# Gated mix of two linear attentions on one core: all projections as seven products of quadrant sums, in three passes over the tokens

## The chip, the cores and the metric

One core of a Trainium2 chip. The metric is the device time of one execution in microseconds (us). Before the change it is 582.25 us, the median of 3 runs (582.17 to 582.32).

## What is computed

x has 2048 tokens of 576 features, all numbers are float32. There are 32 heads of 18. Both branches project x to queries, keys and values, run a linear attention without a mask, and project to 576 outputs; a gate per token mixes the two.

```
g = sigmoid((x * gate_w).sum(-1))
A: q, k, v = x @ A_wqkv;  pq, pk = phi(q), phi(k)      phi(t) = (t > 0 ? t + 1 : exp(t)) + 1e-6
B: q, k, v = x @ B_wqkv;  pq, pk = per head [softmax(t @ w_phi), softmax(-t @ w_phi)]
both:  kv = sum over tokens of pk^T v;  z = sum of pk
       o = (pq @ kv) / (pq . z + 1e-6);  y = o @ wo
out = g * yA + (1 - g) * yB
```

So there are two phases: keys and values of all tokens, then queries and outputs of all tokens.

## The kernel before, in words

**Precision.** Each float32 operand of a projection or output product is split into a high part (rounded to the fast matmul type) and a low part. A product is x_hi W_hi + x_hi W_lo + x_lo W_hi. The 576 features are four chunks of 128 and a tail of 64, whose high and low parts of the weight share the 128 rows of a fifth chunk. One projection is therefore 4 x 3 + 2 = 14 matmuls (`proj`, lines 479 to 486), the token tile (128 x 128) being the loaded operand and up to 512 weight columns the streamed one.

**Tiles and loops.** Tokens are worked in 16 tiles of 128 (`NT`). The branch weights stand in two large tiles `WA` and `WB` (name `WW`), the query weights of B in `W`, those of A in `WW` again; `late` holds the last value columns of both branches (`WR`) and later the normalised queries. `load_x` (426 to 434) loads a token tile and splits it. `keys_values` (584 to 590) computes 1008 columns at once, 512 and 496. `fold_group` (456 to 477) multiplies the per-head map w_phi into B's key or query weights; five groups make a set. `kv_pair` (573 to 579) adds the key-value sums of two tiles in PSUM (name `bk`), 44 small matmuls per branch.

**Order of the stages.** Fold B's key weights and project tiles 0 and 1 in pieces (630 to 656); tiles 2 to 13 in the loop from 660; the last two tiles with their queries (874 to 936); then blocks of two tiles in which query projections (`q_units`), normalisation (`norm_a`, `norm_b`), transposes (`tr_units`), numerators (`num`) and output products (`out_units`) of different tiles are woven (946 to 960). A's key-value map is multiplied into its output weights (`ma_units`, 696 to 722), and the pieces are put together in SBUF by small transfers.

**Who does what.** PE: matmuls and transposes. ACT: copies out of PSUM with rounding, and exponentials. DVE: low parts, maxima, subtractions, sums, reciprocals. POOL: low parts of x, scaling. SP: issues almost all transfers, in order.

**What sets the order.** Operations aren't issued as they are written. A planner (class `Plan`, 139 to 350) records them, gives each a cost (`weigh`, 199 to 230), a due time from the order of the PE work, and picks for each engine the operation with the earliest due time among those that could start soon (`run`, 266 to 339), with the free buffers of each tile name counted in. It then emits them all from line 349, so every instruction in the profile has that line, and groups are told apart by tile names. PSUM holds two tiles of two banks (`pq`), two `tr` and two `bk`.

Of the kernel before, what the change touches and what calls it, by code (L numbers as in the profile page):

```python
# [18 lines left out]
P = 128  # L19
S, D, H, DH = 2048, 576, 32, 18  # L20
NT = S // P
KT = 5
HB = 288
GH = 7
GROUPS = [(g, min(GH, H - GH * g)) for g in range(5)]
NPAIR = 6
# [4 lines left out]
KV = D + 24 * DH  # L31
# [5 lines left out]
class View:  # L37
# [31 lines left out]
    def cells(self):  # L69

        n = math.prod(self.tile.shape[1:])
        first, last = int(self.idx.min()) // n, int(self.idx.max()) // n
        return np.stack([self.idx[0] + (q - first) * n for q in range(first // 32 * 32, last + 1, 32)])
# [23 lines left out]
class Tile:  # L97
    bases = {}

    def __init__(self, pool, shape, dtype, kw):  # L100
        self.pool, self.shape, self.dtype, self.kw = pool, tuple(shape), dtype, kw
        self.psum = pool.psum
# [14 lines left out]
class Pool:  # L117
    def __init__(self, plan, name, real, bufs, psum=False):
        self.plan, self.name, self.real_pool, self.bufs, self.psum = plan, name, real, bufs, psum
# [234 lines left out]
def tile_gated_mix(ctx, tc, xT, wAk, wAv, wBv, wR, wAq, wkT, wqT, phi, woA, woB, out):  # L354
# [9 lines left out]
    ps = Pool(plan, "ps", ctx.enter_context(tc.tile_pool(name="ps", bufs=2, space=bass.MemoryType.PSUM)), 2, True)  # L364

    def r(ap):
        return ap.bitcast(F32)

    def pq_tile():
        return ps.tile([P, 2, 512], F32, name="pq")  # L370

    def tr_tile():
        return ps.tile([P, 512], F32, name="tr")
# [4 lines left out]
    def row_tile():  # L378
        return wk.tile([P, 640], F32, name="row", bufs=6)

    def wraw_tile():
        return wk.tile([P, 640], F32, name="wraw", bufs=3)

    def uw_tile():
        return wk.tile([P, 2, D], F32, name="uw", bufs=3)
# [5 lines left out]
    wr = warm.bitcast(F32R)  # L391
# [26 lines left out]
    z_b = cst.tile([P, 2, D], F32, name="z_b")  # L418
    kb = cst.tile([UB, NB, 64], F32, name="kb")
# [6 lines left out]
    def load_x(t, parts=()):  # L426
        raw = wk.tile([P, 640], F32, name="xraw").rearrange("p (j n) -> p j n", n=P)
        xh = wk.tile([P, KT, P], F32R, name="xh")
        xl = wk.tile([P, KT, P], F32R, name="xl")
        for j in parts or [slice(0, KT)]:  # L430
            SP.dma_start(raw[:, j], xT[t, :, j])
            A.activation(xh[:, j], raw[:, j], AF.Copy)
            (V if parts else G).tensor_tensor(xl[:, j], raw[:, j], r(xh[:, j]), op=ALU.subtract)
        return xh, xl


    def w_tile():
        return wp.tile([P, 9, 578], F32R, name="W", bufs=1)

    def two_tile():  # L440
        return wp.tile([P, 2 * 9 * 578], F32R, name="WW")

    def split(src, hi, lo, eng=V, raw=None):
        raw = (wraw_tile() if raw is None else raw)[:src.shape[0], :src.shape[1]]
        SP.dma_start(raw, src)
        A.activation(hi, raw, AF.Copy)
        a = P - lo.shape[0] if hi.shape[0] == P else 0
        eng.tensor_tensor(lo, raw[a:], r(hi[a:]), op=ALU.subtract)

    def load_w(src, W, n, eng=V, raws=(None,) * KT):  # L450
        for j in range(4):
            split(src[:, j, :], W[:, j, :n], W[:, 5 + j, :n], eng, raws[j])
        split(src[:, 4, :], W[:, 4, :n], W[64:, 4, :n], eng, raws[4])
        return W

    def fold_group(src, W, ph, g, raw=None, tr=False):

        n = GROUPS[g][1] * DH
        rows = P if g < 4 else 80
        raw = wraw_tile() if raw is None else raw  # L460
        SP.dma_start(raw[:rows], src[g, :rows])
        yield
        if tr:
            p1, p2 = tr_tile(), tr_tile()
        else:
            pq = pq_tile()
            p1, p2 = pq[:, 0], pq[:, 1]
        for i in range(KT):
            dst = p1[:, 126 * i:126 * i + n] if i < 4 else p2[:, :n]
            PE.matmul(dst, raw[:n, P * i:P * i + P], ph[:n, 126 * g:126 * g + n], start=True, stop=True)  # L470
        p1v = p1[:, :504].rearrange("p (i c) -> p i c", c=126)[:, :, :n]
        c = slice(126 * g, 126 * g + n)
        A.activation(W[:, 0:4, c], p1v, AF.Copy)
        A.activation(W[:, 4, c], p2[:, :n], AF.Copy)
        V.tensor_tensor(W[:, 5:9, c], p1v, r(W[:, 0:4, c]), op=ALU.subtract)
        V.tensor_tensor(W[64:, 4, c], p2[64:, :n], r(W[64:, 4, c]), op=ALU.subtract)
        yield

    def proj(dst, x, W, c0, n):
        xh, xl = x  # L480
        steps = []
        for j in range(4):
            steps += [(xh, j, j), (xh, j, 5 + j), (xl, j, j)]
        steps += [(xh, 4, 4), (xl, 4, 4)]
        for i, (xx, j, w) in enumerate(steps):
            PE.matmul(dst, xx[:, j, :], W[:, w, c0:c0 + n], start=(i == 0), stop=(i == len(steps) - 1))
# [8 lines left out]
    def phi_elu(pq):  # L495
# [4 lines left out]
        A.activation(fv, pq, AF.Relu, bias=epsc, scale=-1.0)  # L500
        A.activation(fx, fx, AF.Exp, bias=epsc, scale=-1.0)
        V.scalar_tensor_tensor(fv, pq, EPS, fv, op0=ALU.max, op1=ALU.add)
        return f

    def softmax_exp(pq):
        mm = sm.tile([P, 64], F32, name="mm")
        V.tensor_reduce(mm[:, :32], heads(pq), op=ALU.max, axis=AX.X)
        V.tensor_reduce(mm[:, 32:], heads(pq), op=ALU.min, axis=AX.X)
        uw = uw_tile()
# [4 lines left out]
        V.tensor_tensor(v4(0), heads(pq), bc2(mm[:, :32]), op=ALU.subtract)  # L514
        V.tensor_tensor(v4(1), bc2(mm[:, 32:]), heads(pq), op=ALU.subtract)
# [26 lines left out]

    vt = []
    for i in range(4):
        if i < 2:
            v = wk.tile([P, 2, 640], F32, name="ath").rearrange("p a c -> p (a c)")[:, :22 * VC]
            v = v.rearrange("p (a g c) -> p a g c", a=2, c=VC)
        else:
            v = wk.tile([P, 2, 11, VC], F32, name="vo")
        G.memset(v[:, :, 10:, 2 * DH:], 0.0)  # L550
        G.memset(v[:, :, :, 3 * DH:], 1.0)
        vt.append(v)
    kv = [bank_tile(), bank_tile()]

# [3 lines left out]
    def kv_group(t, which, gr, dst, rhs, first):  # L558
        PE.matmul(dst, vt[t % 4][:, which, gr, :], rhs, start=(t == 0 and first), stop=(t == NT - 1), skip_group_check=True)

    def kv_a(t, f):
        for gr, nh in GRP3:
            p, a = divmod(gr, 2)
            kv_group(t, 0, gr, kv[0][64 * a:64 * a + VC, 54 * p:54 * p + DH * nh], f[:, 54 * gr:54 * gr + DH * nh], p == 0)

    def kv_b(t, uw):
        for gr, nh in GRP3:
            p, a = divmod(gr, 2)
            b, o = b_region(p)
            kv_group(t, 1, gr, kv[b][64 * a:64 * a + VC, o:o + 2 * DH * nh].rearrange("p (s c) -> p s c", s=2),  # L570
                     uw[:, :, 54 * gr:54 * gr + DH * nh], p == 1)

    def kv_pair(pend):
        with plan.piece():
            for t, f, _ in pend:
                kv_a(t, f)
            for t, _, u in pend:
                kv_b(t, u)
        pend.clear()

    def evac_v(t, which, src):
        A.activation(vt[t % 4][:, which, :8, :54], src.rearrange("p (g c) -> p g c", c=54), AF.Copy)

    def keys_values(t, x, W, which):

        pq = pq_tile().rearrange("p a c -> p (a c)")
        proj(pq[:, :512], x, W, 0, 512)
        proj(pq[:, 512:KV], x, W, 512, KV - 512)
        evac_v(t, which, pq[:, D:KV])
        return pq[:, :D].rearrange("p (a c) -> p a c", a=2)  # L590

    def last_values(t, x):

        pv = tr_tile()
        proj(pv[:, :HB], x, WR, 0, HB)
        pv = pv[:, :HB].rearrange("p (a c) -> p a c", a=2)
        A.activation(vt[t % 4][:, :, 8:10, :54], pv[:, :, :108].rearrange("p a (g c) -> p a g c", c=54), AF.Copy)
        A.activation(vt[t % 4][:, :, 10, :36], pv[:, :, 108:], AF.Copy)

    def a_part(t, x):  # L600
        return phi_elu(keys_values(t, x, WA, 0))

    def b_part(t, x):
        uw, rs = softmax_exp(keys_values(t, x, WB, 1))
        scale_uw(uw, rs, G)
        last_values(t, x)
        return uw

    xs = {}

    WB, WA = [two_tile()[:, :9 * KV].rearrange("p (j n) -> p j n", j=9) for _ in range(2)]
    WR = wk.tile([P, 2600], F32R, name="late", bufs=1)[:, :9 * HB].rearrange("p (j n) -> p j n", j=9)
# [418 lines left out]
```

## Time and profile before

| | |
|---|---|
| median of 3 runs | 582.25 us |
| the profiled execution | 584.05 us |
| its span, first to last instruction | 582.3 us |
| granted TensorE clock | 1.000 |
| DVE, ACT, POOL busy | 329.7, 230.7, 186.5 us |
| moved by DMA | 29.05 MB |

Groups in the profile read: line, engine, operation, output tile <- input tiles, shapes, count, then busy time, mean of one, and idle time before them with what ended it. Matmul records cover the pipeline from entry to end, so neighbouring records overlap and the means are longer than the distance between two starts.

### The profile page before, as it was taken

Reading aid. Unit: us, or ns where it says so; the run is one execution under the profiler, and the core shown is the slowest. Engines: PE = TensorE matmul, PEld = TensorE weight load, DVE = VectorE, ACT = ScalarE, POOL = GpSimd, SP = SyncE. Lnnn points to the kernel's source line nnn. Section 1 sums busy time; section 2 is a strip of 40 time slices with the busy share of each in tenths; the row PEclk is TensorE's granted clock in tenths of the full one; section 3 lists DMA queues with packets and bytes.
Section 4 is the critical chain, followed back from the end, with each engine's and each line's share of the span. In section 5 each row is a group of like instructions: output and inputs, shape, how many; then the busy total and the mean of one; then the engine's idle time right before and its main releaser. Section 6 shows DMA issues by size and latency. Waiting matters only on the chain.

```text
span 582.3 us, 10081 instructions
## 1 busy us (share of the span) xinstructions
PE 574.1 (99%) x4180; PEld 522.5 (90%) x4180; DVE 329.7 (57%) x553; ACT 230.7 (40%) x486; POOL 186.5 (32%) x154
## 2 busy tenths in 40 slices
PE   7999999999999999999999999999999999999997
PEld 7978888888888888888889899999999999999997
DVE  3951443324333332353479998777778787787610
ACT  4643332323333231324366543535444444533531
POOL 4031221212222121247264664342334333333200
PEclk9999999999999999999999999999999999999999
DMA  8631101111000000002144101011011010000001
GB/s 296 213 106 44 46 24 24 35 44 43 26 23 24 12 14 21 24 25 82 46 112 131 57 22 44 24 44 44 20 45 44 24 44 22 21 22 20 4 38 42
DMA packets 15014, 29.05 MB, mean 50 GB/s; under 512 B 2508, under 2 KB 4812, under 8 KB 14968
## 3 DMA queue, kind: packets, MB, share of 16 engines
q1 hardware_dynamic: 14824, 28.33, 15.9%
q8 instruction: 33, 0.54, 0.4%
q14 instruction: 13, 0.11, 0.1%
q10 hardware_dynamic: 144, 0.06, 0.0%
HBM read 22.65 MB, written 4.72 MB: 47 GB/s over the span
## 4 chain that ended last, share of the span: by engine, by line
PE 89%; DVE 4%; DMA 4%; ACT 2%; SPq 1%; issue 0%
PE pq L349 52%; PE bk L349 25%; PE tr L349 12%; DMA row<-wkT 1%; DMA wraw<-wAk 1%; ACT WW L349 1%; DVE late L349 1%; DVE WW L349 1%; SPq L349 1%; DMA wraw<-wAv 1%; DVE den L349 1%; DMA wraw<-woB 1%; DVE mm L349 0%; DVE uw L349 0%; DVE row L349 0%
## 5 line engine op out<-in xcount | busy, mean ns | idle before, releaser
L349 PE MATMUL pq<-WW,xh 128*128 128x512 f32 (+3 forms) x864 | 243.7, 358 | 0.3 <-DVE WW L349 0.3
L349 PEld LDWEIGHTS pq<-WW,xh 128*128 128x128 f32 x864 | 153.1, 188 | 21.5 <-DVE WW L349 0.8
L349 PE MATMUL pq<-WW,xl 128*128 128x512 f32 (+3 forms) x480 | 169.7, 356 | 0.0
L349 POOL TENSOR_TENSOR xl<-xraw,xh 128x640 fp32r<-128x640 f32 x30 | 47.0, 1566 | 177.4 <-ACT xh L349 175.4
L349 PEld LDWEIGHTS pq<-WW,xl 128*128 128x128 f32 x480 | 90.4, 188 | 12.0
L349 DVE TENSOR_REDUCE mm<-pq 128x32 f32<-128x576 f32 x64 | 45.6, 752 | 85.5 <-ACT vo L349 43.8
L349 PE MATMUL bk<-WW,vo 128*128 128x288 f32 x480 | 70.8, 296 | 0.0
L349 PEld LDWEIGHTS bk<-WW,vo 128*128 128x128 f32 x480 | 65.8, 188 | 0.0
L349 PE MATMUL pq<-W,xh 128*128 128x288 f32 x288 | 63.2, 303 | 0.0
L349 DVE SCALAR_TENSOR_TENSOR row<-pq,row 128x576 f32<-128x576 f32 x32 | 24.1, 753 | 67.5 <-ACT ath L349 23.8
L349 DVE TENSOR_REDUCE ss<-uw 128x64 f32<-128x1152 f32 x32 | 43.1, 1348 | 26.3 <-ACT uw L349 26.2
L349 PE MATMUL bk<-WW,ath 128*128 128x288 f32 x256 | 55.9, 305 | 0.0
L349 POOL TENSOR_TENSOR uw<-uw,rs 128x1152 f32<-128x1152 f32 x16 | 34.4, 2154 | 48.6 <-DVE rs L349 48.6
L349 PEld LDWEIGHTS pq<-W,xh 128*128 128x128 f32 x288 | 47.3, 189 | 0.5
L349 ACT ACTIVATE row<-pq,epsc 128x576 f32<-128x576 f32 x32 | 23.8, 744 | 58.2 <-PE pq L349 58.2
L349 ACT ACTIVATE uw<-uw 128x1152 f32<-128x1152 f32 x32 | 37.3, 1165 | 23.8 <-DVE uw L349 23.8
L349 PE MATMUL pq<-W,xl 128*128 128x288 f32 x160 | 46.5, 296 | 0.0
L349 PEld LDWEIGHTS bk<-WW,ath 128*128 128x128 f32 x256 | 40.6, 188 | 2.7 <-issue 2.7
L349 ACT ACTIVATE uT<-tr 118x512 f32<-118x512 f32 (+1 forms) x44 | 24.6, 564 | 44.0 <-PE tr L349 44.0
L349 POOL TENSOR_TENSOR row<-row,den 128x378 f32<-128x378 f32 (+1 forms) x32 | 29.4, 939 | 36.7 <-DVE den L349 29.5
L349 POOL TENSOR_TENSOR row<-uw,z_b 128x576 f32<-128x576 f32 x18 | 26.6, 1482 | 40.3 <-ACT uw L349 23.1
L349 PE MATMUL bk<-WW,atl 128*128 128x288 f32 x128 | 37.7, 294 | 0.0
(119 smaller groups left out, 822.5 us busy)
## 6 DMA issues: line engine op xcount, KB each, us to landing
xraw<-xT SPq DMA_DIRECT2D x30, 320.0 KB
out<-row SPq DMA_DIRECT2D x15, 288.0 KB
wraw<-woB SPq DMA_DIRECT2D x6, 288.0 KB
wraw<-wAq SPq DMA_DIRECT2D x5, 289.0 KB
wraw<-wAk SPq DMA_DIRECT2D x5, 288.0 KB
wraw<-woA SPq DMA_DIRECT2D x5, 288.0 KB
wraw<-wqT SPq DMA_DIRECT2D x4, 320.0 KB
wraw<-wkT SPq DMA_DIRECT2D x3, 320.0 KB
```

The costliest lines, as they stand in the source:

```text
L349: fn(*[a.real() if isinstance(a, View) else a for a in args], **{k: v.real() if isinstance(v, View) else v for k, v in kw.items()})
```

## The change

1. **Seven products.** Tokens are taken in pairs of tiles (t1, t2), features in two halves of 256 and the tail of 64, columns in two matrices k and v (keys and values, or B's and A's queries). A pair's result is a 2 x 2 block product, and `strassen` computes it in seven products of sums of quadrants, accumulated in three PSUM tiles X, Y, Z. The tail is multiplied plainly in four products. Each product runs over two halves of 288 columns (290 in pass A, whose extra columns hold the gate). Kept partial sums are copied out of X by ACT (`keep`) and added to Y or Z by DVE.
2. **Three passes.** Pass A: keys and values of branch A for all tokens, tiles 0 and 1 in the plain form. Pass B: keys and values of branch B. Pass Q: queries of both branches with normalisation, transposes, numerators and output. Each pass uses the operand set of its own; during a pass the next pass's set is prepared (`set_ops`): differences of quadrants, split in high and low. Three of a set's seven operands go through DRAM and are loaded when tiles come free (11 tiles `op`).
3. **x.** `x_prep` (pass A) forms the quadrant sums of x, splits them and stores them in DRAM; `x_load` (passes B, Q) loads them again and splits the plain parts afresh. The tiles xu, xv, xp, xq have one buffer each.
4. **Output weights** are split or computed in pass B, put together in DRAM (`WO_d`) by transfers, and loaded as four `op` tiles and a `tail` in pass Q.
5. **Buffers.** Three `pq` tiles in place of two; `tr` is gone (in pass Q one `pq` tile takes its part); 8 `row` tiles, 2 `uw` tiles. Key-value sums of A and B are separate pieces (`kv_a`, `kv_b`). Planner costs are as they were.
6. **Engines.** The subtractions of the first softmax of a pair are on POOL in pass Q; feature maps and softmaxes read sums in SBUF instead of PSUM in three of the four quadrants in pass Q, and in one of two in passes A and B.

```diff
-        raw = wk.tile([P, 640], F32, name="xraw").rearrange("p (j n) -> p j n", n=P)
...
+    def x_prep(n, raw, sums):
+        x, (xu, xv, xp, xq) = x_tiles()
+        r1, r2 = chunks(raw[:, 0]), chunks(raw[:, 1])
+        s2, s1, s3, s4 = [sums[:, 2 * i:2 * i + 2] for i in range(4)]
+        A.activation(xu[:, 0], r1, AF.Copy)
+        G.tensor_tensor(xu[:, 1], r1, r(xu[:, 0]), op=ALU.subtract)
...
+        V.tensor_tensor(s1, r2[:, 0:2], r2[:, 2:4], op=ALU.add)
+        V.tensor_tensor(s2, s1, r1[:, 0:2], op=ALU.subtract)
...
+        SP.dma_start(XP_d[n], r(xp))
+        SP.dma_start(XQ_d[n], r(xq))
...
+    def x_load(n):
+        for t, src, k in ((xu, xT[2 * n], 5), (xv, xT[2 * n + 1, :, 2:], 3)):
+            raw = chunks(wk.tile([P, 640], F32, name="raw", bufs=1)[:, :P * k])
+            SP.dma_start(raw, src)
+            split(raw, t[:, 0], t[:, 1], G)
+        SP.dma_start(r(xp), XP_d[n])
+        SP.dma_start(r(xq), XQ_d[n])
...
+    def op_steps(x, w):
+        return [s for j in range(2) for s in ((x(0, j), w[:, j]), (x(0, j), w[:, 2 + j]), (x(1, j), w[:, j]))]
+    def tail_steps(x, w):
+        return [(x(0, 0), w), (x(1, 0), w)]
+    def strassen(x, W, T, n, c1_tile, c11, c22, c21, c12):
+        X = pq_tile()
+        mul(X, op_steps(x["11"], W[1]), True)
+        c1 = pair(c1_tile())
+        keep(c1, X, n)
+        Y = pq_tile()
+        mul(Y, op_steps(x["12"], W[2]) + tail_steps(x["t1"], T[:, 0]), True)
+        V.tensor_tensor(c1, c1, Y[:, :, :n], op=ALU.add)
+        c11(c1)
+        mul(X, op_steps(x["s2"], W[6]), False)
+        keep(c2, X, HB)
+        Z = pq_tile()
+        mul(Z, tail_steps(x["t2"], T[:, 1]) + op_steps(x["s1"], W[5]), True)
+        mul(X, op_steps(x["s3"], W[7]), False)
+        keep(c3, X, HB)
+        c22(c3, Z)
+        mul(X, op_steps(x["22"], W[4]) + tail_steps(x["t2"], T[:, 0]), False)
+        c21(X)
+        mul(Z, op_steps(x["s4"], W[3]) + tail_steps(x["d"], T[:, 1]), False)
+        c12(c2, Z)
...
+    def b_sinks(n, uws, pend):
+        t1, t2 = 2 * n, 2 * n + 1
+        return (lambda c: softmax_k(t1, c, uws[0], V, pend), lambda c, Z: v_add(t2, c, Z),
+                lambda X: softmax_k(t2, X[:, :, :HB], uws[1], V, pend), lambda c, Z: v_add(t1, c, Z))
...
+        for i, _ in enumerate(strassen(x, WB, TB, D // 2, lambda: uws[0][:, 0], *b_sinks(n, uws, pend))):
+            if i == 3 and n + 1 < NT // 2:
+                x_next = x_load(n + 1)
+            if i == 4:
+                if n:
+                    kv_b(done)
+                else:
+                    kv_a(a_done)
+            if n or i > 4:
+                steps(prep)
...
+    def q_units(n, x, uws, c1_tile, mid=None, end=None):
+        def c11(c):
+            qb[t1] = softmax_exp(c, uws[0], G)
+        def c22(c, Z):
+            V.tensor_tensor(c, c, Z[:, :, :HB], op=ALU.add)
+            qa[t2] = phi_elu(c)
+        def c21(X):
+            qb[t2] = softmax_exp(X[:, :, :HB], uws[1])
+        def c12(c, Z):
+            V.tensor_tensor(c, c, Z[:, :, :HB], op=ALU.add)
+            qa[t1] = phi_elu(c)
```

More of the change, by code (lines that the diff above doesn't have):

```diff
@@ L437, in w_tile @@
[L437 to L454, printed above, removed]
@@ L479, in proj @@
[L479 to L486, printed above, removed]
+    XP_d = [dr.tile([P, 2, 4, P], F32, name=f"xp{n}") for n in range(NT // 2)]
+    XQ_d = [dr.tile([P, 2, 5, P], F32, name=f"xq{n}") for n in range(NT // 2)]
@@ new lines, in load_ops, with folds, load @@
+    def load_ops(W, Wd, x):
+        for op in (7, 4, 3):
+            W[op] = op_tile()
+            plan.first = ()
+            SP.dma_start(r(W[op]), Wd[op])
+    def folds(src, K, ph, raw, ahead):
+        SP.dma_start(ph, phi.rearrange("p a c -> p (a c)"))
+        def load(g):
+            rows = P if g < 4 else 80
+            rw = raw()
+            SP.dma_start(rw[:rows], src[g, :rows])
+            return rw
+        nxt = load(0)
+        yield
+        for g, nh in GROUPS:
+            n = nh * DH
+            rw, nxt = nxt, load(g + 1) if g < 4 and ahead else None
+            pq = pq_tile()
+            for i in range(KT):
+                dst = pq[:, 0, 126 * i:126 * i + n] if i < 4 else pq[:, 1, :n]
+                PE.matmul(dst, rw[:n, P * i:P * i + P], ph[:n, 126 * g:126 * g + n], start=True, stop=True)
+            if g < 4 and not ahead:
+                nxt = load(g + 1)
+            c = slice(126 * g, 126 * g + n)
+            A.activation(K[:, 0:4, c], pq[:, 0, :504].rearrange("p (i c) -> p i c", c=126)[:, :, :n], AF.Copy)
+            A.activation(K[:, 4, c], pq[:, 1, :n], AF.Copy)
+            yield
@@ L672, in widths, with kv_group, kv_order, kv_a @@
-    def widths(p):
-        return [(a, DH * GRP3[2 * p + a][1]) for a in range(2) if 2 * p + a < len(GRP3)]
+    def kv_group(t, gr, dst, rhs, first):
+        PE.matmul(dst, vt[t % 4][:, gr, :], rhs, start=(t == 0 and first), stop=(t == NT - 1), skip_group_check=True)
+    def kv_order(t):
+        return [GRP3[g ^ (t % 2 if g < 10 else 0)] for g in range(11)]
+    def kv_a(pend):
+        with plan.piece():
+            for t, f in pend:
+                for gr, nh in kv_order(t):
+                    p, a = divmod(gr, 2)
+                    kv_group(t, gr, kv[0][64 * a:64 * a + VC, 54 * p:54 * p + DH * nh], f[:, 54 * gr:54 * gr + DH * nh], p == 0)
@@ new lines, in kv_b, with steps @@
+    def kv_b(pend):
+        with plan.piece():
+            for t, uw in pend:
+                for gr, nh in kv_order(t):
+                    p, a = divmod(gr, 2)
+                    b, o = b_region(p)
+                    kv_group(t, gr, kv[b][64 * a:64 * a + VC, o:o + 2 * DH * nh].rearrange("p (s c) -> p s c", s=2),
+                             uw[:, :, 54 * gr:54 * gr + DH * nh], p == 1)
+    def steps(gen, n=1):
+        for _ in range(n):
+            next(gen, None)
+    raw = at_tile([2, 640])
@@ new lines, in tile_gated_mix, with tmp_rows @@
+    (k1, s1), (k2, s2) = plain(1, 2, 0, 0), plain(1, 2, 0, 1)
+    for i in range(0, 10, 2):
+        run(s1[i:i + 2])
+        run(s2[i:i + 2])
+    pend = []
+    for t, k in enumerate((k1, k2)):
+        pend.append((t, phi_elu(k[:, :, :HB])))
+        gate_of(t, k[:, 0, HB:HB + 1])
+    for t in range(2):
+        v, s = plain(12, 3, 1, t)
+        run(s)
+        v_copy(t, v)
+    x_load_raw(1, raw)
+    x = x_prep(1, raw, sums)
+    def tmp_rows():
+        return row_tile()[:, :2 * HG], row_tile()[:, :2 * HG]
@@ new lines, in islice_pair, with drams @@
+    def islice_pair(u):
+        return u[:, 0], u[:, 1]
+    def drams(name):
+        return {op: dr.tile([P, 4, D], F32, name=f"{name}{op}") for op in (7, 4, 3)}
+    WB, WBd, TB = {}, drams("wb"), tail_tile()
+    prep = prep_b()
+    for n in range(1, NT // 2):
+        done, pend = pend, []
+        x_next = None
+        for i, _ in enumerate(strassen(x, WA, TA, HG, row_tile, *a_sinks(n, pend))):
+            if i == 0 and n < NT // 2 - 1:
+                x_load_raw(n + 1, raw)
+            if i == 2 and n < NT // 2 - 1:
+                x_next = x_prep(n + 1, raw, sums)
+            if i == 4:
+                kv_a(done)
+            steps(prep)
+        x = x_next
@@ L675, in runs @@
+    steps(prep, 99)
+    x = x_load(0)
+    load_ops(WB, WBd, x)
+    spare = [at_tile([2048]) for _ in range(2)]
+    more = [s[:, :2 * D].rearrange("p (s n) -> p s n", s=2) for s in spare]
+    ph = spare[1][:, 2 * D:2 * D + 630]
+    rawq = spare[0][:, 2 * D:2 * D + 640]
+    WO_d = dr.tile([P, 2, 9, D], F32, name="wod")
+    MA_d = dr.tile([198, 2, D], F32, name="mad")
     def runs(size):
@@ new lines, in tile_gated_mix, with load_out, WO @@
+    steps(prep, 99)
+    x = x_load(0)
+    load_ops(WQ, WQd, x)
+    def load_out(x):
+        flat = WO_d.rearrange("p s i n -> p (s i) n")
+        for k in range(4):
+            t = op_tile()
+            plan.first = x["dma"][:1]
+            SP.dma_start(r(t), flat[:, 4 * k:4 * k + 4])
+            WOt.append(t)
+        t = tail_tile()
+        plan.first = x["dma"][:1]
+        SP.dma_start(r(t), flat[:, 16:18])
+        WOt.append(t)
+    WOt = []
+    def WO(s, i):
+        c = 9 * s + i
+        return WOt[c // 4][:, c % 4]
@@ new lines, in chain, with end0 @@
+    def chain(*gens):
+        for g in gens:
+            yield from g
+    UBS = []
+    def end0():
+        fold_b()
+        UBS.extend([late[:, 0], late[:, 1]])
+    late = wide_tile(1, [2, 1300])
+    late = late.rearrange("p a c -> p a c")[:, :, :UB * NB]
+    uT = wide_tile(0, [NB, 256])
+    b_done = pend
+    extra_uw = wk.tile([P, 2, D], F32, name="vo")
+    for _ in q_units(0, x, [uw_tile(), uw_tile()], row_tile, lambda: kv_b(b_done), end0):
+        pass
+    blocks = [{} for _ in range(NT // 2 + 3)]
@@ new lines, in tile_gated_mix @@
+    for i in range(NT // 2 + 1):
+        while norms:
+            norms.pop(0)()
+        cur, prev = blocks[i], blocks[i - 1]
+        seqs = []
+        if i and i <= NT // 2:
+            prev["ot"] = num(uT, prev["at"], i >= NT // 2 - 1)
+        if i + 1 < NT // 2:
+            x = x_load(i + 1)
+            if i == 0:
+                load_out(x)
+            uws = [extra_uw if i == 0 else uw_tile(), uw_tile()]
+            seqs.append((7, .7, q_units(i + 1, x, uws, row_tile)))
+        ts = (2 * i + 1, 2 * i)
+        if i < NT // 2:
+            at = at_tile([2, 4, 256], F32R)
+            cur["at"] = (at[:, 0], at[:, 1])
+            seqs.append((8, 1, chain(*[tr_units(t, cur["at"], uT) for t in ts])))
+        if i:
+            seqs.append((4, 1, chain(*[out_units(t, prev) for t in (2 * i - 1, 2 * i - 2)])))
+        merge(*seqs)
```

676 lines of the change are left out of this document (348 added, 328 removed).

## The prediction

> **What bounds the kernel now.** I read the page's busy times first, then the windows over whole periods, then the groups of matmuls, then single rows of the timeline.
>
> ```profile
> PE 574.1 (99%) x4180; PEld 522.5 (90%) x4180; DVE 329.7 (57%) x553; ACT 230.7 (40%) x486; POOL 186.5 (32%) x154
> PE 89%; DVE 4%; DMA 4%; ACT 2%; SPq 1%; issue 0%
> ```
>
> PE is busy for 574.1 of 582.3 us, and 89% of the chain that ended last runs through it. A busy PE is a modelled figure, so I ask the windows whether it works at a steady rate. The first row below is a pair of token tiles in the keys-and-values stage, the second a pair in the query stage (columns: window, then PE, PEld, DVE, ACT, POOL busy with counts, clock, DMA share, GB/s).
>
> ```profile
> 102.70:135.80 33.10, 33.10 (x240) 28.72 (x239) 11.49 (x17) 10.87 (x20) 7.03 (x4) 1.00 0.11 29
> 401.60:437.20 35.60, 35.60 (x278) 34.26 (x274) 27.91 (x49) 16.03 (x38) 12.48 (x11) 1.00 0.11 36
> ```
>
> No idle PE, full clock, DVE at 35% in the first and 78% in the second. So the time is PE's queue of work, and removed PE work comes off the end only if the other four engines keep up with a faster PE.
>
> **The change, part by part.**
>
> *Projection matmuls.* The groups, by shape:
>
> ```profile
> L349 PE MATMUL pq<-WW,xh 128*128 128x512 f32 x270 | 88.6, 398 | 0.3 <-DVE WW L349 0.3
> L349 PE MATMUL pq<-WW,xh 128*128 128x496 f32 x270 | 85.1, 387 | 0.0
> L349 PE MATMUL pq<-W,xh 128*128 128x288 f32 x288 | 63.2, 303 | 0.0
> L349 PE MATMUL pq<-WW,xl 128*128 128x512 f32 x150 | 59.0, 393 | 0.0
> L349 PE MATMUL pq<-WW,xl 128*128 128x496 f32 x150 | 58.1, 387 | 0.0
> L349 PE MATMUL pq<-W,xl 128*128 128x288 f32 x160 | 46.5, 296 | 0.0
> L349 PE MATMUL pq<-WW,xh 128*128 128x288 f32 x180 | 38.1, 297 | 0.0
> L349 PE MATMUL pq<-WW,xh 128*128 128x290 f32 x144 | 32.1, 305 | 0.0
> L349 PE MATMUL tr<-late,xh 128*128 128x288 f32 x144 | 30.3, 296 | 0.0
> L349 PE MATMUL pq<-WW,xl 128*128 128x288 f32 x100 | 28.9, 295 | 0.0
> L349 PE MATMUL pq<-WW,xl 128*128 128x290 f32 x80 | 23.7, 301 | 0.0
> L349 PE MATMUL tr<-late,xl 128*128 128x288 f32 x80 | 23.0, 294 | 0.0
> ```
>
> Their means overlap (a matmul's record covers its pipeline), so I price by the distance between starts. The first column of these timeline rows is the start.
>
> ```profile
> 13.49 0.51 PE L349 MATMUL pq<-WW,xh 128*128 128x288 f32 x2
> 21.00 0.55 PE L349 MATMUL tr<-WW,xh 128*128 128x432 f32 x2
> 26.55 0.42 PE L349 MATMUL tr<-late,xh 128*128 128x288 f32 x2
> 61.97 0.62 PE L349 MATMUL pq<-WW,xh 128*128 128x512 f32 x2
> 68.34 1.28 PE L349 MATMUL tr<-row,wraw 126*128 126x126 f32 x10
> ```
>
> From 13.49 to 21.00 stand four sets of 14 matmuls of 288 columns: 7.51/56 = 0.1341 us each. From 61.97 to 68.34 stand 14 of 512 and 14 of 496: 6.37/28 = 0.2275 us. From 21.00 to 26.55 stand 28 of 432: 5.55 us. The two prices give 0.432 ns a column and about 9.6 ns a matmul.
>
> Before: 840 wide ones are 30 sets of 6.37 = 191.1; 28 of 432 are 5.5; 1176 of 288 or 290 are 157.7, and two more columns on 224 of them 0.2. Sum 354.5 us.
>
> After: a pair of tiles needs, per pass, 7 products of 6 steps by 2 halves, and 4 tails of 2 steps by 2 halves: 84 + 16 = 100 matmuls of 288 or 290 columns. The plain form in the same width is 2 tiles by 14 steps by 4 = 112. Eight pairs by three passes is 24, of which the first is plain: 23 x 100 + 112 = 2412, which is also the count in the changed kernel's own instructions (812 of 290, 1600 of 288). 2412 x 0.1341 + 0.7 = 324.2 us. **Minus 30.3 us.** One product in eight would be 12.5%; the tails, which are not saved, and the narrower matmuls leave 8.5%.
>
> A rule against it: the Trainium skill, TensorE: Matmul & The Clock Gate, section Back-to-back issue gap, gives for sustained streams about 81 ns at 128 columns and 131 ns at 512, so that wide matmuls would be far cheaper per column. By that rule, interpolated, the projections would go from about 230 to about 246 us, an estimate, and the change would lose 13 us or so. The trace does not agree: 227.5 ns against 134.1.
>
> *Start.*
>
> ```profile
> 4.75 2.34 PE L349 MATMUL pq<-row,wraw 126*128 126x126 f32 x10
> 11.27 1.31 PE L349 MATMUL pq<-row 72*128 72x72 f32 x10 [0.60 <-DMA row<-wkT]
> 12.41 1.32 PE L349 MATMUL tr<-row 126*128 126x126 f32 x10
> 4.00:6.00 2.00, 2.00 (x10) 2.00 (x10) 0.00 (x0) 0.00 (x0) 1.19 (x8) 1.00 1.01 361
> 6.00:8.00 2.00, 1.09 (x6) 0.80 (x4) 0.08 (x1) 0.76 (x2) 0.00 (x0) 1.00 1.01 384
> ```
>
> Before, five fold groups (11.27 to 12.41 is 1.14 us each, 5.7 us in all) come first, and projections begin at 13.49. After, the first work is the plain product of pair 0, whose 112 matmuls take 15.0 us. The first load lands at about 4.7 (the 4.75 row), and two splits of about 0.7 us on ACT follow, so it starts near 6.2. Its keys need 2.1 MB, which at 361 to 384 GB/s is in by 8, so PE sets the pace. The folds come back later as 5.7 us of PE work. Net: -13.5 + 6.2 + 5.7 = **-1.6 us**, between -2.5 and +2 (if the splits, not PE, pace it).
>
> *Switches of matmul kind.*
>
> ```profile
> 379.87 0.60 PE L349 MATMUL tr<-ident,late 128*118 128x128 f32 x4
> 380.23 0.51 PE L349 MATMUL pq<-WW,xh 128*128 128x290 f32 x2
> 380.58 0.29 PE L349 MATMUL pq<-WW,xl 128*128 128x290 f32 x1
> 380.71 0.43 PE L349 MATMUL pq<-WW,xh 128*128 128x290 f32 x2
> 380.97 0.30 PE L349 MATMUL pq<-WW,xl 128*128 128x290 f32 x1
> ```
>
> Two matmuls after transposes take 0.35 us (380.23 to 380.58), two in the stream 0.26: a switch costs 0.09. The key-value sums now stand in 16 pieces where 8 stood (A's and B's in different passes), 16 more switches: **+1.4 us**. Transposes, numerators, output products and their counts are unchanged.
>
> So without any new wait: 582.25 - 30.3 - 1.6 + 1.4 = **551.7 us**. The profiled execution took 584.05, its span 582.3; I apply differences to the median of the runs, 582.25.
>
> *New waits.* Nothing in the old trace shows them, so I bound them.
>
> What must now be hidden: per pair, three additions of a kept sum to PSUM (in Q) or one and two value additions (in B), six ACT copies out of PSUM, operand preparation for the next pass on DVE, POOL and ACT, and x re-read through SP's queue (236 transfers in place of 124).
>
> ```profile
> L349 DVE TENSOR_TENSOR uw<-pq,mm x32: 741/749/758, 23.4 to 533.8; 128x576 f32<-128x576 f32 x32
> L349 DVE TENSOR_REDUCE ss<-uw x32: 1293/1353/1354, 33.5 to 536.4; 128x64 f32<-128x1152 f32 x32
> L349 DVE RECIPROCAL rs<-ss x32: 495/545/554, 36.0 to 539.8; 128x64 f32<-128x64 f32 x32
> L349 ACT ACTIVATE uw<-uw x32: 1147/1168/1170, 28.1 to 535.2; 128x1152 f32<-128x1152 f32 x32
> L349 POOL TENSOR_TENSOR uw<-uw,rs x16: 2147/2154/2159, 36.7 to 273.0; 128x1152 f32<-128x1152 f32 x16
> L349 DVE TENSOR_TENSOR late<-uw,rs x42: 222/716/1874, 311.4 to 550.1; 128x540 f32<-128x540 f32 x28, 128x72 f32<-128x72 f32 x14
> L349 DVE SCALAR_TENSOR_TENSOR rs<-den,gg,rs x16: 183/274/1382, 311.0 to 548.0; 128x64 f32<-128x64 f32 x16
> 256.65 2.29 PE L349 MATMUL bk<-uw,ath 128*55 128x108 f32 x43
> ```
>
> Pass Q: a pair's PE time falls to 35.60 - 12 x 0.1341 = 34.0. DVE's rises from 27.9 by three additions of 0.75 and falls by two subtractions of 0.75 that go to POOL: 28.7, or 84%. Pass B: PE has 100 x 0.134 + 2.3 = 15.7 us a pair. DVE has the old stage's 11.5 without two feature maps (1.5) and with 2.6 of additions: 12.6, or 80%, and some 10% for preparation. Pass A is lighter. DVE still has room everywhere, but its queue is in order.
>
> The tightest place is the chain of the second softmax of a pair in B: two reductions and two subtractions (3.0), exp (1.17), sum and reciprocal (1.9), POOL's scaling (2.15), semaphores about 0.8: 9.0 us from the sixth product's end to the key-value sums. These stand behind the seventh product and five of the next pair, 2.1 + 1.6 + 2.1 + 1.6 + 2.1 + 1.6 = 11.1 us later. Two us of slack, with a DVE queue of about 1 us in front. Queued behind a waiting sum is every later matmul.
>
> In numbers: first Strassen pair (its operand sums run 8 us on DVE after the last weight load) 3, B 3, the seams where 3.5 MB of operands and 5.3 MB of output weights must land beside x 2, Q and its filling 2. **+10 us**, with bounds of 0 (the old trace has no such idle time) and 24 (1 us a pair and pass; the rival below goes further). Forecast: 551.7 + 10 = **562 us**.
>
> **The rivals.**
>
> 1. *No new wait at all*: 550 to 553. For it: both windows above show a scheduled PE without idle time, one with DVE at 78%. Against it: five engines now exchange three accumulators a pair. Chance 0.10.
> 2. *Waits at the seams and in B that are twice my estimate* (operands and x through one queue, the 9 us chain late by 1 to 2 us a pair): +20 to 26, so 572 to 578. Chance 0.20.
> 3. *The gain is eaten by DVE and POOL standing in each other's way*, the case on the other side. In the rows above, operations with a PSUM operand hardly vary (741 to 758 ns), while those with both operands in SBUF do: 716 to 1874, 274 to 1382, collisions of about 1.1 us. The change adds SBUF-sourced ones (the first softmax, the feature maps) and raises POOL's instructions from 154 to about 235. If 7 of some 14 such operations a pair collide in Q, DVE gets 28.7 + 7.7 = 36.4 us a pair, more than PE's 34.0, and with 5% of queueing of its own 38.2: +4.2 by 8. In B the chain loses another 1 us a pair: +8. With the other 5: 551.7 + 34 + 8 + 5 = 599 us. It decides against the change from 1.3 us a pair and pass on (30.5/24). Against it: the averages in the windows contain the old collisions, and half of all colliding is far from the mean of the same rows. Chance 0.17. The Trainium skill, SBUF — State Buffer, section Who interferes with whom, says that a DVE instruction with two SBUF inputs and a GpSimd instruction that reads SBUF exclude each other for a whole instruction; the rows' spread agrees.
> 4. *The work doesn't shrink*: 2412 matmuls in place of 2044. Columns fall by 78,200, worth 33.8 us at 0.432 ns, and 368 more matmuls eat that up if the fixed part of one is 92 ns; by the two start distances it is 9.6. If the whole price were per matmul, 354.5 us would become 418. Chance 0.01, counted with the slower ones.
>
> **How the numbers follow.** Forecast 0.50 (faster), rival 1 0.10 (faster), rival 2 0.20 (faster), rivals 3 and 4 0.18 (slower), and 0.02 for waits that happen to cancel the gain. A measurement of this kernel tells about 0.2%, 1.2 us, from no change. Faster 0.80, same 0.02, slower 0.18. The range leaves out the fastest end of rival 1 and most of rival 3: 551 to 584 us.
>
> **What would show it.** Right: the groups of 288 and 290 count 2412 with starts 0.134 apart; a pass Q pair of 34 to 35 us with DVE near 29; idle PE of about 10 us beside the start. Rival 3: DVE's two-SBUF operations with means well above 0.82 us and PE idle behind DVE in Q. Rival 2: PE waiting on DMA for the operand or output weight tiles, or on POOL ahead of the key-value sums in B. Wrong altogether: a start distance above 0.14, or projections that begin later than 9 us.

## The result, and the profile after

The changed kernel takes **637.53 us** (median of 4 runs, 635.57 to 640.72), the kernel before 582.29 beside it: a ratio of 1.0954, 95% interval 1.0904 to 1.1005. The forecast was 562, the range 551 to 584. The profiled execution took 640.72 us, its span 638.9. Of e1 below, one run of four is left out, which took 636.05 us at a granted clock of 0.844.

The page after: busy times, the granted clock in 40 slices of 16 us, the chain that ended last.

```profile
PE 576.6 (90%) x4548; PEld 537.6 (84%) x4548; DVE 420.4 (66%) x652; ACT 294.0 (46%) x589; POOL 299.7 (47%) x236
...
PEclk9989999999995998999999999989999999999999
...
PE 63%; DVE 17%; ACT 6%; DMA 6%; issue 4%; POOL 2%; SPq 1%; ACTq 0%; POOLq 0%; DVEq 0%
```

PE has 368 more matmuls, as counted beforehand, but is busy for 90% of the span where it was 99%, and the clock dips, which it never did before. The view of PE's waits (total us, times, longest) names who ends the idle time:

```profile
PE pq L350 <- ACT row L350: 31.3, 56, 3.1
PE pq L350 <- DMA xq<-xq: 6.4, 1, 6.4
PE pq L350 <- DVE vo L350: 5.5, 6, 1.9
PE pq L350 <- DMA at<-wqT: 2.3, 1, 2.3
...
PE pq L350 <- ACT gate L350: 1.8, 7, 0.3
```

All rows of that view add up to 58 us (4 in the kernel before). The mean clock of 0.981 over 638.9 us is at most another 12; the part of it that falls into idle time costs nothing.

**The wait that comes 56 times.** A stretch of pass A in the timeline, PE first, then ACT (start, length, instruction, count, idle time before it):

```profile
107.35 1.51 PE L350 MATMUL pq<-op,xu 128*128 128x290 f32 x10
109.36 1.34 PE L350 MATMUL pq<-op,xu 128*128 128x290 f32 x8 [0.50 <-ACT row L350]
...
111.89 1.63 PE L350 MATMUL pq<-op,xp 128*128 128x290 f32 x11
114.02 0.40 PE L350 MATMUL pq<-op,xp 128*128 128x290 f32 x1 [0.50 <-ACT row L350]
```

```profile
108.89 0.41 ACT L350 ACTIVATE row<-pq 128x290 f32<-128x290 f32 x1 [0.60 <-PE pq L350]
...
113.55 0.41 ACT L350 ACTIVATE row<-pq 128x288 f32<-128x288 f32 x1 [0.73 <-PE pq L350]
```

A product is 6 matmuls for each half (bank) of X. The first half's copy could start after the sixth matmul, at about 108.2. It starts at 108.89, when the tenth is through, and the eleventh, which writes only the other half, starts behind the copy's end. By 0.134 us a matmul it was due at 108.69: 0.67 us are lost, 0.50 of them shown as idle time; the other 0.17 I put down to the draining and refilling of the matmul pipeline.

**The seam between passes A and B.** SP's queue, then PE:

```profile
173.28 2.44 SPq L350 DMA_DIRECT2D row<-row  x3
175.84 0.40 SPq L350 DMA_DIRECT2D row<-woB  x1
176.28 0.75 SPq L350 DMA_DIRECT2D row<-row  x1
177.08 0.51 SPq L350 DMA_DIRECT2D wod<-row  x1
177.63 7.61 SPq L350 DMA_DIRECT2D row<-row  x10
185.34 0.46 SPq L350 DMA_DIRECT2D row<-woB  x1
185.90 0.85 SPq L350 DMA_DIRECT2D wod<-row  x2
186.84 0.44 SPq L350 DMA_DIRECT2D row<-woB  x1
187.37 0.71 SPq L350 DMA_DIRECT2D xq<-xq  x1
```

```profile
186.21 2.31 PE L350 MATMUL bk<-at,vo 128*55 128x108 f32 x44
194.90 2.98 PE L350 MATMUL pq<-op,xq 128*128 128x288 f32 x11 [6.38 <-DMA xq<-xq]
```

Fourteen small copies that lay out A's key-value map by heads (`row<-row`, 1 to 11 KB) cost SP about 0.76 us each (7.61 for the ten in a row). The load of xq for the next pair stands behind them, and PE idles 6.4 us.

**The start.** DVE and POOL beside the first seven-product pair:

```profile
26.85 1.97 DVE L350 TENSOR_TENSOR row<-late,row 128x580 f32<-128x580 f32 x1
28.75 3.75 DVE L350 TENSOR_TENSOR op<-row,op 128x580 fp32r<-128x580 f32 x2
...
37.71 0.75 DVE L350 TENSOR_TENSOR row<-uT,row 128x580 f32<-128x580 f32 x1
```

```profile
28.16 1.79 POOL L350 TENSOR_TENSOR xp<-at,xp 128x512 fp32r<-128x512 f32 x1
29.92 1.95 POOL L350 TENSOR_TENSOR row<-late 128x580 f32<-128x580 f32 x1
31.83 1.94 POOL L350 TENSOR_TENSOR op<-row,op 128x580 fp32r<-128x580 f32 x1
```

The same kind of DVE operation takes 0.75 us when POOL rests (as it does from 36.5 to 40.8 us) and about 1.9 while POOL works.

### The profile page after: what moved, and what is told of

The parts are those of the page before. It is cut to its first block, busy times and chain, and to the rows that moved or that the text cites. A ratio compares the mean times of both kernels' runs of the same rounds, so it can differ in the third digit from the quotient of the medians.

```text
span 638.9 us, 11489 instructions
## 1 busy us (share of the span) xinstructions
PE 576.6 (90%) x4548; PEld 537.6 (84%) x4548; DVE 420.4 (66%) x652; ACT 294.0 (46%) x589; POOL 299.7 (47%) x236
## 4 chain that ended last, share of the span: by engine, by line
PE 63%; DVE 17%; ACT 6%; DMA 6%; issue 4%; POOL 2%; SPq 1%; ACTq 0%; POOLq 0%; DVEq 0%
PE pq L350 48%; PE bk L350 15%; DVE row L350 4%; ACT row L350 4%; DVE dd L350 2%; DVE den L350 2%; DVE vo L350 2%; POOL row L350 1%; DVE ss L350 1%; DVE at L350 1%; DMA xq<-xq 1%; DVE late L350 1%; DMA at<-wqT 1%; DMA late<-wAv 1%; DVE rs L350 1%
## 5 line engine op out<-in xcount | busy, mean ns | idle before, releaser
L350 PE MATMUL pq<-op,xq 128*128 128x288 f32 (+1 forms) x552 | 95.7, 309 | 15.1 <-ACT row L350 8.6
L350 PE MATMUL pq<-op,xu 128*128 128x288 f32 (+1 forms) x600 | 100.6, 307 | 9.0 <-ACT row L350 6.7
L350 PE MATMUL pq<-op,xp 128*128 128x288 f32 (+1 forms) x552 | 91.3, 301 | 10.9 <-ACT row L350 10.1
L350 PEld LDWEIGHTS pq<-op,xu 128*128 128x128 f32 x600 | 86.6, 193 | 15.6 <-ACT row L350 8.5
L350 PEld LDWEIGHTS pq<-op,xq 128*128 128x128 f32 x552 | 81.2, 195 | 20.1 <-ACT row L350 19.5
L350 PEld LDWEIGHTS pq<-op,xp 128*128 128x128 f32 x552 | 78.2, 189 | 15.9 <-ACT row L350 14.8
L350 PE MATMUL bk<-op,vo 128*128 128x288 f32 x480 | 72.1, 302 | 0.1
L350 PEld LDWEIGHTS bk<-op,vo 128*128 128x128 f32 x480 | 67.2, 192 | 0.3 <-DVE vo L350 0.3
L350 PE MATMUL bk<-op,at 128*128 128x288 f32 x320 | 62.6, 300 | 0.0
L350 PE MATMUL pq<-op,xv 128*128 128x288 f32 (+1 forms) x300 | 55.3, 313 | 7.0 <-ACT row L350 5.2
```

The lines of the kernel that those rows point to most:

```text
L350: fn(*[a.real() if isinstance(a, View) else a for a in args], **{k: v.real() if isinstance(v, View) else v for k, v in kw.items()})
```

## The experiments

Three theories: **T1**, the copies of X between its halves; **T2**, queues blocked by the small copies and by late weight loads; **T3**, DVE and POOL at the start and in the filling of pass Q (its first pairs, when its stages are not all at work yet). The rivals to T1 were that the copy's own length is waited for, and that DVE already sets the pace. Times are medians. e2, e4, e5 and all that build on e5 contain e1's edit, except e14; what each builds on stands in its diff.

### The copies of X: e1_keep, e2_keep_gate, e7_piece

```diff
         def keep(dst, acc, w):
-            for hf in range(2):
-                A.activation(dst[:, hf], acc[:, hf, :w], AF.Copy)
+            A.activation(dst, acc[:, :, :w], AF.Copy)      # e1
+            with plan.piece(): (the old loop)               # e7
...
     def gate_of(t, src):
+        plan.after(1)                                       # e2: behind the feature map
```

> The copy of the running product X out of PSUM (keep) becomes one ACT instruction over both halves instead of one for each half. Theory T1 (dependencies follow the whole tile of two banks: the copy of half 0 waits for half 1's matmuls that were already issued, and half 1's last matmuls wait for the copy of half 0, about 0.75 us for each of 24 x 3 keeps): 637.5 -> about 590 us (583 to 600), a pair of pass A 17.8 -> about 15.4 us, a pair of pass Q 37.1 -> about 34.8, and PE's waits for ACT 'row' from 31 + 52 us to under 15. Rival R1 (the copy itself is what PE waits for, since X is used again two products later): the one copy ends later than the two did (0.6 us in place of 2 x 0.41, and begun later), so the time stays at 632 to 645 and the waits stay. Rival R2 (my rival 3: DVE's and POOL's operations stretch each other and DVE sets the pace): PE's waits move from ACT to DVE, the gain stays under 15 us, DVE's busy share of a pair in pass Q is over 90%.

> As e1_keep, and the gate's copy of one column (128x1, from the same PSUM tile or row) is ordered behind the feature map of its token tile instead of ahead of it or between. T1: 3 to 4 us less than e1_keep (7 waits of 0.26 us shown and the drain beside each). R1 and R2: within 1 us of e1_keep.

> The changed kernel with its two copies of X for each keep, still two ACT instructions, but planned as one piece, so that both stand behind the matmuls of both halves. T1 (what costs is that a copy of one half stands between the matmuls of the other half of the same tile): as e1_keep, 606 to 616 us, and waits of PE for ACT 'row' under 10 us. Rival (the saving of e1_keep came from 69 fewer ACT instructions): 630 to 640 us.

e1: **610.55** (ratio to the kernel before 1.0486, 1.0464 to 1.0507), above the 583 to 600 of T1 and far below the rivals. e2: **609.32**. e7: **615.61** (1.0584, 1.0541 to 1.0627), in the span that T1 gave and far from its rival's: what counts is where the copies stand, not how many there are. (One wait of 5.4 us in e7, for POOL ahead of the key-value sums, is not among e2's.) In e2 PE's waits for ACT 'row' are down from 31.3 to this, and others have opened:

```profile
PE pq L350 <- DMA xq<-xq: 7.2, 1, 7.2
PE pq L350 <- DVE vo L350: 6.4, 6, 2.1
PE pq L350 <- DVE row L350: 6.2, 4, 3.9
PE pq L350 <- DMA at<-wqT: 5.6, 2, 5.3
PE pq L350 <- ACT row L350: 4.9, 6, 1.9
```

Both rivals to T1 fall. The time fell by 27 us where I had expected 47. In e2 PE's waits for anything but ACT 'row' rose from 27 to 37 us, so part of the gain was spent there; e14_halves below measures the copies with those waits mended. The gate's copy gave 1.2 where 3 to 4 were expected, within the scatter of a microsecond or two.

### The seams: e3_kg_act, e4_both, e5_seams, e8_kg_late

```diff
-            SP.dma_start(KG[...], KA[...])
+            A.dma_start(KG[...], KA[...])                   # e3, e4 (e4 = e2 and this)
```

> The changed kernel with the 14 small copies KA to KG in DRAM-to-SBUF order issued from ACT's queue instead of SP's. Theory T2 (SP's queue stood 12 us behind these copies, so the stored sums xq of the second pair of pass B landed at 194.8 us, PE idled 6.4 us and the clock then fell to 0.50 for 10 us): 637.5 -> 624 to 628 us, no idle PE over 2 us between 185 and 200, clock over 0.9 there. Rival (SP's time is that of the whole queue, the reads of output weights among it, so xq is late anyway): 634 to 640, and the same wait for xq.

> e2_keep_gate and e3_kg_act together. If the two causes lie in different stretches their gains add: about 575 us (568 to 590). If a third thing bounds both (R2), less than the sum by over 8 us.

e3: **647.93**, 10 us slower than the changed kernel and outside both spans that I had given. e4: **608.11**, no better than e2, where 575 was expected. T2 as I had put it fell. e4's ACT queue shows why:

```profile
156.15 11.62 ACTq L350 DMA_DIRECT2D row<-row  x14
167.86 0.52 ACT L350 ACTIVATE xv<-raw 128x384 fp32r<-128x384 f32 x1 [12.27 <-DMA row<-row]
```

A copy takes 0.83 us of ACT's queue as it took 0.76 of SP's. On ACT the fourteen hold up all that stands behind them, the exponentials too, and PE now waits 6.1 us for ACT 'uw'. So the copies have to be spread, not moved.

```diff
# e5 (on e2), e8 (on e5)
-        for h0, h1 in runs(3):
+        for i, (h0, h1) in enumerate(runs(3)):              # e5: two to a step
...
+            if i % 2:
+                yield
...
-        yield from folds(wqT, kr, ph, lambda: rawq, False)
+        yield from folds(wqT, kr, ph, row_tile, True)       # e5: load one step ahead
# e8: the copies behind the loads of woB, and 800 ns of SP for each in weigh()
```

e5 also leaves the gates of the first pair in their old order.

> e2_keep_gate (gate order only from the second pair on) with the 14 small copies two to a step, still on SP's queue, and the folds of the query weights loading one step ahead into two row buffers. T2, mended (moving the copies to ACT's queue only moved the block, since each takes about 0.8 us of the queue that issues it; in e2_keep_gate this and the late query load cost 7.2 + 5.6 us of idle PE and 7 us of lower clock): 609 -> 583 to 592 us, no wait over 2 us between 140 and 240. Rival (the queue is full over the whole stretch, so that the waits turn up elsewhere): 600 to 610.

> e5_seams with the 14 small copies behind the loads of the gated output weights (two to a step) and counted by the planner at 0.8 us of SP each instead of 0.4. In e5_seams the planner had bunched them after all (8 in 6.04 us, 5 in 3.84 us): a weight load stood behind them, ACT stood behind that weight's split, and the copy of X that PE waited for stood behind it on ACT: 5.7 us idle and 3.4 us of lower clock. T2: these go, 599 -> 588 to 592 us. Rival (the row buffers, held longer by the two matrices, become what PE waits for): 595 or more.

e5: **599.21** (less 10; 22 expected). The wait for the query weights is gone. That for xq became one for ACT, 5.7 us long; SP and ACT in e5:

```profile
164.32 3.84 SPq L350 DMA_DIRECT2D row<-row  x5
168.26 0.46 SPq L350 DMA_DIRECT2D row<-woB  x1
```

```profile
171.35 0.68 ACT L350 ACTIVATE row<-row 128x576 fp32r<-128x576 f32 x1 [8.22 <-DMA row<-woB]
...
173.08 0.65 ACT L350 ACTIVATE row<-pq 128x576 f32<-128x576 f32 x1
```

The planner had bunched the copies again, a weight load came behind them, its split blocked ACT, and PE waited for the copy of X queued behind that split. e8: **592.34** (1.0161, 1.0141 to 1.0181), at the edge of the 588 to 592 that T2 gave and under its rival's 595. Together the seams cost 17 us of 609, the late query weights and the lower clock included.

### The start and the filling: e6_plain1, e9 to e13

```diff
# e6 (on e5): the second pair also in plain form, eight products
# e9 (on e8): at the start x_prep's and set WA's operations on V instead of G
-        put(WA, 5, j, t1, G)
+        put(WA, 5, j, t1, V)
# e10 (on e8), e11 (on e9): no step of pass B's preparation in the first such pair
+            if n > 1:
                 steps(prep)
# e12 (on e11)
-            norm_b(t, *qb[t], ub, (G, V, G if t < 4 else V))
+            norm_b(t, *qb[t], ub, (G, G, G) if t < 4 else (G, V, V))
# e13 (on e12): operands 5, 7, 4 of the first set split only behind the first copy of X;
#   the remainders of pair 0's token sums on V instead of G (two operations)
+            plan.first = [kept]
             put(WA, 5, j, t1, V)
```

> e5_seams, and the second pair of pass A also in eight products, so that the sums of the operands have some 15 us more. T3 (DVE and POOL stretch each other at the start and the first seven-product pair waits for them, 6.6 us of idle PE and 2 us of clock): 28 more matmuls cost about +2.7 us and the waits of 8 us go: 5 us less than e5_seams, about 582 us. Rival (the same DVE and POOL work is only put off and PE waits for it later): 1 to 4 us more than e5_seams.

> e8_kg_late, and between the first and the second pair of pass A every two-SBUF operation on DVE, none on POOL (sums of the weights and of the tokens, and their remainders). Theory T3 (an operation on DVE and one on POOL exclude each other, so that two of them take 2.0 us side by side, while two on DVE alone take 2 x 0.75): the mean of DVE's 128x580 operations between 16 and 40 us falls from about 1.9 to 0.8 us, the wait of 3.9 us for DVE 'row' shrinks to under 2, 2 to 6 us less than e8_kg_late. Rival (DVE's queue is simply full there): the wait grows, 2 to 6 us more.

> e8_kg_late with the weights of pass B begun one pair of tokens later (no fold in the first seven-product pair). T3: in that pair DVE, POOL and the three two-bank tiles are all taken, and the first folds stand in PE's queue ahead of products that could run; 3 to 5 us less, 592 -> 587 to 589. Rival (PE waits for the same DVE row with or without the folds): 591 to 593.

> e9_start_dve with the same delay. In e9 the wait for DVE was gone, but 2.9 us were spent in a fold that waited for its weights and 1.1 in another for a tile: 594 -> 587 to 590 by T3. Rival: 593 to 595.

> e11_both, and in the first two pairs of pass Q one more 128x576 product and the scaling on POOL instead of DVE. In the filling of pass Q DVE is busy 19 of 20 us and PE idles some 9 us. If DVE's count of operations sets the pace: 2 to 3 us less than e11_both. If the exclusion of DVE and POOL does (two at a time take the sum of both): within 1 us of it, or slower.

> e12_fill, and at the start of pass A the operands of products 5, 7 and 4 are split only behind the first copy of X (in e12_fill that copy stood on ACT behind splits that waited for DVE: 3.9 us of idle PE and 1.7 us of lower clock), and the remainders of the first pair's token sums on DVE. If the start's loss is one of order on ACT: 589 -> 583 to 586. If DVE's own work sets it: 588 to 590, and the wait only changes its name.

e6: **603.15**, 4 more than e5: the rival was right, PE waited 5.3 us for DVE one pair later. (A plain pair has 12 matmuls more, 112 against 100, not the 28 of the expectation.) e9: **594.42** against 592.34. The first half of its expectation held, DVE in e9 at the start:

```profile
24.27 0.76 DVE L352 TENSOR_TENSOR op<-row,op 128x580 fp32r<-128x580 f32 x1
24.95 0.82 DVE L352 TENSOR_TENSOR xu<-at,xu 128x640 fp32r<-128x640 f32 x1
25.68 0.76 DVE L352 TENSOR_TENSOR op<-row,op 128x580 fp32r<-128x580 f32 x1
```

The stretching is gone, and with it the wait of 3.9 us; waits of 2.2 us for ACT and 2.9 for a weight load took its place, so it paid nothing that can be told. The Trainium skill, SBUF — State Buffer, section Who interferes with whom, lets such a DVE instruction and a reading GpSimd one only run one after the other; the 1.9 against 0.76 us agree.

e10: **593.42**, near the rival's 591 to 593, against T3's 3 to 5 us less. e11: **591.56**, 2.9 under e9 and between its two spans; the runs of the two overlap (590.73 to 593.96 against 592.26 to 596.6). In e11 PE still waited 3.95 us, now for ACT, which stood in splits that waited for DVE. e12: **589.06**, 2.5 less. It moved one product in each of four tiles, about 3 us of DVE (the scaling that its expectation names was on POOL already). So DVE's count of operations sets the pace in the filling, as the expectation had it. Windows over the filling, e11 then e12 (after PE and PEld come DVE, ACT, POOL):

```profile
300.00:350.00 50.00, 42.40 (x287) 37.70 (x286) 47.59 (x81) 25.56 (x55) 37.63 (x35) 0.97 0.39 141
```

```profile
300.00:350.00 50.00, 44.71 (x299) 39.48 (x299) 44.47 (x75) 27.24 (x56) 38.72 (x37) 0.97 0.36 130
```

e13: **581.79**, 7.3 less, better than the 583 to 586 expected. The wait of 3.9 us for ACT and that of 2.1 for DVE are gone, which fits a loss of order on ACT's queue once POOL was out of DVE's way. But e13 changed two things, the order and the engine of two remainders, and no run tells them apart. Against the kernel before its ratio is 0.999 (0.9973 to 1.0006): no difference that can be told.

### The copies again, alone: e14_halves, and e15_ahead

```diff
# e14 (on e13): the old loop over hf in keep
# e15 (on e13)
-            SP.dma_start(src, woB[:, i, :])
+            src, nxt = nxt, load_b(i + 1) if i < 5 else None
```

> e13_start with one thing undone: X is copied in two halves again, as in the changed kernel. It measures T1's price with the other waits gone. By the gaps and the drains counted between the changed kernel and e2_keep_gate (17 us of idle PE and 15.6 us of matmul starts in 24 x 3 copies): 30 to 36 us more than e13_start. If the halves only cost where other things were late as well: under 20 us.

> e13_start with the gated output weights loaded one step ahead of their split. In e13_start the largest wait left in pass B is 2.2 us for ACT 'row' in its first pair, ACT standing in a split whose load had just been issued. If this is again a load issued too late: that wait goes and the time is 578 to 580.5 us, under the kernel before. If SP's queue is full there whatever the order: 581 to 583.

e14: **618.71**, 36.9 more than e13, just over the 30 to 36 expected. For 23 x 3 copies (pair 0 is plain, the 24 in the expectation was one too many) that is 0.53 us each. In e1 only 27 of it showed; the 10 us by which the other waits grew in e2 would be the rest. A pair of pass Q in e13, then in e14:

```profile
402.90:437.70 34.80, 34.02 (x260) 32.53 (x260) 26.62 (x48) 16.66 (x33) 13.98 (x12) 1.00 0.20 67
```

```profile
433.70:470.70 37.00, 35.00 (x260) 32.62 (x260) 27.88 (x48) 17.15 (x36) 14.19 (x12) 1.00 0.19 63
```

e15: **584.63** (1.0062, 1.0035 to 1.0088), 2.8 more than e13 and above both its spans: earlier loads did not pay, 2.0 us for ACT 'row' stayed and one of 1.7 came. No version here beats the kernel before.

## Why the prediction was wrong, step by step

- **Matmuls and their price: right; the saving on the whole: almost a third short.** Matmuls of 288 and 290 columns still start 0.134 us apart, and 2412 of them stand in the three passes. But my sum took 30.5 us off PE's work. Without idle PE, the span before is 578 us (582.3 less 4.4) and e13's 557 (578.5 less 21.7): 21 less. Of the 9 missing, restarts would make some 5, by an estimate of 0.17 us as above behind each of e13's 32 waits; where the rest went is not shown.
- **Pass Q's pair: right, but for the copies.** 34.0 was forecast, 34.8 is e13's, 37.1 the changed kernel's; DVE's 27.9 there is under the 28.7 forecast.
- **Start: half right.** Projections began at 5.17 (forecast 6.2), but the plain pair ended at 25.4, not 21.2. PE waited 0.8 us for a split on ACT and 1.4 for a feature map on DVE. And from 6.8 to 11.3 us its matmuls started some 0.24 us apart, not the 0.134 of my sum, which costs about 2 us. Why is not shown; the profile's clock row has no dip there.

```profile
7.47 1.17 PE L350 MATMUL pq<-op,xu 128*128 128x290 f32 x4
8.44 1.17 PE L350 MATMUL pq<-op,row 128*128 128x290 f32 x4
...
11.89 0.97 PE L350 MATMUL pq<-op,xu 128*128 128x290 f32 x6
12.70 0.96 PE L350 MATMUL pq<-op,xv 128*128 128x290 f32 x6
```

- **The step that failed: "New waits: +10 us", bounds 0 to 24.** In the changed kernel PE was idle for 58 us (4 before) and lost up to 12 by a lower clock. The span less both is 569, some 12 over e13's 557; restarts of the matmul stream would account for it, which was not measured by itself. Its terms:
  - The copies between the halves: 36.9 us by e14. I counted "six ACT copies" as work of ACT with room to spare. I did not ask where the queue put each copy, nor who stands behind it. It stood in the sum at nothing; that is the largest miss, and no rival had it.
  - The seams, 2 us in my sum: 17 by e2 to e8. I saw that operands must land, but summed megabytes, and not the 0.76 us that SP needs for a copy of a few KB.
  - The first pair, 3 us: about 8 from e8 to e13 (592.3 to 581.8, less e12's 2.5), nearly all of it in e13.
  - Q and its filling, 2 us: e12 got back 2.5, and in e13 7.7 us of idle PE between 300 and 370, and 0.8 a pair after that, are left.
  - B, 3 us: its softmax chain was in time; the view of PE's waits has only one ahead of a matmul into `bk`, 1.3 us at the very start.
- **Rivals.** Rival 2's mechanism (one queue for operands and x) was real at the seam, 17 us; its other half, the chain in B, was not. Rival 3's (DVE and POOL exclude each other) was real at the start; in pass Q DVE needed 27.9 us a pair, not the rival's 36.4, and the two-SBUF operations suffer little, as two groups of the changed kernel show (busy, mean ns; the second has one of 1997 ns and a median of 759). Its time, 599, was nearer than mine, but not for its reason.

```profile
L350 DVE TENSOR_TENSOR late<-uw,rs 128x540 f32<-128x540 f32 x24 | 17.4, 727 | 0.9
...
L350 DVE TENSOR_TENSOR row<-uw,z_b 128x576 f32<-128x576 f32 x15 | 13.3, 887 | 0.8 <-ACT z_b L350 0.8
```

That the copies wait because a dependency is kept for the whole tile of two banks is argued from the order in the timeline; e7 and e14 show that the place of the copies costs the time, not why they were held up there.

## What to carry to other kernels

Where an accumulator is copied out in parts, look at which instruction of the producer stands behind each copy on its queue: one copy behind the whole product was 37 us cheaper here than two that start earlier. Price a new transfer by what it takes of the queue that issues it as well as by bytes, and ask who stands behind it, on each queue it could be moved to. Removed PE work is worth its price only where every other queue keeps its order: here the span without idle PE fell from 578 to 557 us, and with most of the waits mended the time came back only to where it had been.

## What the hardware showed that I had not expected

The granted clock can halve after idle time. Windows of the changed kernel: the wait for xq, the 14 us from its last part on, and the stretch after.

```profile
188.52:194.90 6.38, 0.00 (x0) 0.03 (x1) 0.00 (x0) 3.06 (x5) 1.40 (x1) 0.79 0.98 329
192.00:206.00 14.00, 10.10 (x39) 9.43 (x40) 4.48 (x7) 3.98 (x6) 6.49 (x4) 0.51 0.79 287
206.00:220.00 14.00, 12.48 (x81) 11.07 (x80) 9.08 (x14) 6.15 (x11) 5.56 (x4) 1.00 0.77 259
```

The clock of 0.5 lasted for 13.7 us, of which 2.7 lay in the wait (0.79 over 6.38 us) and 11 behind its end, with PE at work: the 6.4 us of idle time cost about 5.5 us more. The other dips of this run lasted 3.4, those of the experiments 3.4, 6.8 or 10.2. The Trainium skill, TensorE: Matmul & The Clock Gate, section What's actually happening, gives half rate after an idle window of about 3.4 us; the lengths here are multiples of that. The waits ahead of them can be shorter, and there the measurement decides. In e15 this one was followed by 3.4 us at 0.50, from 164.45 on:

```profile
163.22 2.28 PE L352 MATMUL pq<-op,xq 128*128 128x288 f32 x12 [1.96 <-ACT row L352]
```

In e13, whose longest wait is 2.2 us, the clock stayed at 1.00 until the end. So a wait of about 2 us may or may not bring a dip; which it is, no run here settles.
